# Squares added on GpSimd in pieces of 256 columns, for five head pairs in place of three

## The chip, the core and the metric

The kernel runs on one core of a Trainium2 chip. The metric is the time of one execution on the device in microseconds (us). Five engines work side by side, each through its own list of instructions in order, and wait for each other by semaphores: TensorE (PE in the rows; PEld is its weight load), VectorE (DVE), ScalarE (ACT), GpSimd (POOL) and SyncE (SP), which issues most of the DMA transfers. SBUF is the memory on the core, PSUM holds what TensorE writes.

## The reference

Three layers follow each other. The change lies in the hand-over from the first to the second.

```python
scores = scale * np.matmul(q, k.transpose(0, 1, 3, 2))   # 2 batches, 8 heads, 768 positions, 64 per head
scores = np.where(keep, scores + bias, -1e9)             # window of 96 back, 8 global keys
a = np.exp(scores - max); a = a / (a.sum(-1) + 1e-9)
attn_out = a @ v

x = attn_out.transpose(0, 2, 1, 3).reshape(1536, 512)    # a row: one position, 8 heads of 64
rms = np.sqrt(np.mean(x * x, axis=-1) + 1e-6)            # over the 512 columns of a row
xn = x / rms * rms_g
y = (silu(xn @ w_gate) * (xn @ w_val)) @ w_out           # 512 -> 1536 -> 512

# third layer: tokens routed to one of 8 experts (512 -> 1024 -> 512, relu), added to y
```

`mean(x * x)` is the sum that the change regroups: for each position the squares of 512 numbers are added.

## The kernel before, in words

**Attention.** Work is cut into 24 items: 8 head pairs `pr` (two heads of one batch; `pr` 0 to 3 are batch 0, 4 to 7 batch 1), each with three groups `g` of 256 positions. The generator `attention` runs 28 steps `t`; in step t five items are in flight, each in another stage. For item t (`a`) TensorE multiplies q by k (L243) and VectorE adds the bias and finds the maximum (`ttr`, L254, four instructions); ScalarE takes the exponential with its sum z (`exp`, L265, four). For item t - 1 (`b`) VectorE adds 1e-9 to z and takes the reciprocal (`zadd`, L270; `zrec`, L274) and GpSimd scales the four parts of `es` (`norm`, L282; in step 24, the last with an item `b`, VectorE does it). For item t - 2 (`c`) TensorE transposes (L289), and VectorE and ScalarE copy the result out of PSUM (L298, L300). For item t - 3 (`d`) TensorE multiplies by v (L324). For item t - 4 (`e`) `out` calls `Rms.take`.

**Squares.** `Rms.take` gets 128 partitions (the two heads' 64 columns of x, transposed) by 256 positions. ScalarE scales and rounds them into `xh` (L428), squares them into a third of a tile `sq` of 128 x 768 (L429), and VectorE makes the remainder `xl` (L430). A batch has four such tiles, one for a head pair. The sum over a row's 512 columns is one over 128 partitions and four tiles. `stats` makes it on TensorE: a matmul of a block of 128 positions of `sq` against a column of ones (L458), one for each block and each tile left in the list `self.sq`, 6 blocks in a batch. Each such matmul stands in the trace as two records. `add` (L436) takes the second tile off that list and adds it into the first on GpSimd, 128 x 768 at once; the loop at L401 does it at the end of steps 11, 14 and 23 (head pairs 1, 2 and 5). So batch 0 has two tiles left for `stats`, batch 1 three.

**What follows.** `stats` of batch 0 stands in step 17, of batch 1 in steps 26 and 27. `root` (L461) turns the sums into 1/rms on VectorE in small instructions, one after each of VectorE's other instructions (`tick`); `spread` (L488) brings them to all partitions by TensorE. From step 13 on, one step of a generator `unit` (L498 on) prepares weights of the second layer: ScalarE (L503), VectorE (L505, L510, L512, L515, one in a step), ScalarE (L517) and GpSimd (L518, the low part `wl`). In steps 25, 26 and 27 TensorE begins the second layer's first matmuls (L552).

**Order.** The schedule is by hand: each engine does its instructions in the order in which the program writes them. `sq` has four buffers, which the tiles `rd` of `root` share; a tile's buffer is free when nothing in the program uses it any longer.

Of the kernel before, what the change touches and what calls it, by code (L numbers as in the profile page):

```python
# [15 lines left out]
ALU = mybir.AluOpType  # L16
# [11 lines left out]
def f(ap):  # L28
    return ap.bitcast(F32)
# [162 lines left out]
def attention(s, rms):  # L192
# [11 lines left out]
    def tick():  # L204
        next(s.small, None)


    def load(pr):
        q = qs[pr] = ap.tile([128, 768], F32, name="qd", bufs=3)
        ks[pr] = ap.tile([128, 928], F32, name="kd", bufs=3)  # L210
        if pr:
            nc.sync.dma_start(q, s.qx[pr])
            nc.sync.dma_start(ks[pr], s.kx[pr])
            return
        for a, b, c, d in ((0, 256, 0, 288), (256, 768, 288, 928)):
            nc.sync.dma_start(q[:, a:b], s.qx[pr, :, a:b])
            nc.sync.dma_start(ks[pr][:, c:d], s.kx[pr, :, c:d])

    def loadv(pr):
        v = vs[pr] = ap.tile([128, 2, 11, 64], F32, name="vp", bufs=3)  # L220
        nc.sync.dma_start(v.rearrange("p h b d -> p (h b d)"), s.vx[pr, :, 0:1408])
        lo, hi = halves[pr % 3]
        nc.sync.dma_start(lo[0:64].rearrange("p h b d -> p (h b d)"), s.vx[pr, 0:64, 1408:2176])
        nc.sync.dma_start(hi[64:128].rearrange("p h b d -> p (h b d)"), s.vx[pr, 64:128, 1408:2048])
# [8 lines left out]
    def qk(it, t):  # L233
        pr, g = it

        sc = [s.ps_g.tile([128, 2, 256], F32, name=f"sc{x}", tag=f"ps{x}", bufs=2) for x in range(2)]
        for r in range(2):
            for h, x in ((0, 0), (1, 1), (0, 1), (1, 0)):
                k0, _, _, n = part(g, r, x)
                d = slice(64 * h, 64 * h + 64)  # L240
                o = slice(64 * (h ^ x), 64 * (h ^ x) + 64)
                i = 128 * (2 * g + r) + 64 * x
                nc.tensor.matmul(sc[x][o, r, 0:n], lhsT=qs[pr][d, i:i + 64],  # L243
                                 rhs=ks[pr][d, k0:k0 + n], start=True, stop=True)
        m = ap.tile([128, 4], F32, name="m", bufs=4)
        z = ap.tile([128, 4], F32, name="z", bufs=4)
        st[it] = (sc, es[t % 3], m, z)

    def ttr(it, r, x):

        pr, g = it
        sc, e, m, z = st[it]
        _, b0, e0, n = part(g, r, x)
        nc.vector.tensor_tensor_reduce(  # L254
            out=e[:, r, e0:e0 + n], in0=sc[x][:, r, 0:n], in1=s.bias[:, pr % 4, b0:b0 + n],
            scale=-0.125, scalar=3.0e38, op0=ALU.add, op1=ALU.min,
            accum_out=m[:, 2 * r + x:2 * r + x + 1])

    def exp(it, r):
        pr, g = it  # L260
        sc, e, m, z = st[it]
        for x in range(2):
            _, _, e0, n = part(g, r, x)
            j = 2 * r + x
            nc.scalar.activation(e[:, r, e0:e0 + n], e[:, r, e0:e0 + n], AF.Exp,  # L265
                                 bias=m[:, j:j + 1], scale=-1.0, accum_out=z[:, j:j + 1])

    def zadd(it):
        z = st[it][3]
        nc.vector.tensor_scalar(z, z, 1e-9, None, ALU.add)  # L270

    def zrec(it):
        z = st[it][3]
        nc.vector.reciprocal(z, z)  # L274

    def norm(it, r, x, eng):
        pr, g = it
        sc, e, m, z = st[it]
        _, _, e0, n = part(g, r, x)
        j = 2 * r + x  # L280
        one = (1.0, ALU.mult) if eng is nc.gpsimd else (None,)
        eng.tensor_scalar(e[:, r, e0:e0 + n], e[:, r, e0:e0 + n], z[:, j:j + 1], one[0], ALU.mult, *one[1:])  # L282

    def trans(it, r):
        pr, g = it
        e = st[it][1]
        pt = s.ps_n.tile([128, 3, 128], F32, name="pt", tag="rb", bufs=2)
        for k in range(1 if g == r == 0 else 0, 3):
            nc.tensor.transpose(pt[:, k, :], e[:, r, 128 * k:128 * k + 128], s.ident)  # L289
        pts = ap.tile([128, 3, 128], F32, name="pts", bufs=4)  # L290
        outs[it, r] = (pt, pts)

    def evac(it, r, eng):
        pr, g = it
        pt, pts = outs[it, r]
        k = slice(1 if g == r == 0 else 0, 3)
        if eng is nc.vector:
            nc.vector.tensor_copy(pts[:, k], pt[:, k])  # L298
        else:
            nc.scalar.copy(pts[:, k], pt[:, k])  # L300

    def pv(it, r):
        pr, g = it
        pts = outs.pop((it, r))[1]

        if r == 0:
            po = s.bank([128, 512], "po")
            outs[it] = po[:, 0:256].rearrange("p (a b) -> p a b", a=2)
            s.spare = po[:, 256:512]
        po = outs[it]  # L310
        i = 2 * g + r
        lo, hi = halves[pr % 3]

        def terms(hh):
            a, b = slice(64 * hh, 64 * hh + 64), slice(64 - 64 * hh, 128 - 64 * hh)
            yield 0, 1, lo[:, hh, i], a
            if i:
                yield 0, 0, vs[pr][:, hh, 2 * i - 1], a
                yield 1, 1, hi[:, hh, i - 1], b
            yield 1, 2, vs[pr][:, hh, 2 * i], b  # L320

        for n, two in enumerate(zip(terms(0), terms(1))):
            for hh, (x, k, v, c) in enumerate(two):
                nc.tensor.matmul(po[64 * hh:64 * hh + 64, r, 64 * x:64 * x + 64], lhsT=v,  # L324
                                 rhs=pts[:, k, c], start=i == 0 or n % 2 == 0, stop=i == 0 or n % 2 == 1)

    def out(it):
        pr, g = it
        po = outs.pop(it)
        rms[pr // 4].take(pr % 4, g, po.rearrange("p a b -> p (a b)"))  # L330
# [15 lines left out]
    for t in range(n + 4):  # L346
        a, b, c, d, e = (items[t - z] if 0 <= t - z < n else None for z in range(5))
        if a:
            qk(a, t)
        if c:  # L350
            trans(c, 0)
            trans(c, 1)
        if d:
            pv(d, 0)
            pv(d, 1)
        if b:
            zadd(b)
            tick()
            zrec(b)
            tick()  # L360
            if t < n:
                for r in range(2):
                    for x in range(2):
                        norm(b, r, x, nc.gpsimd)
            else:
                norm(b, 1, 1, nc.vector)
                norm(b, 0, 0, nc.vector)
            tick()
        if a:
            ttr(a, 0, 0)  # L370
            tick()
        if b and t >= n:
            norm(b, 0, 1, nc.vector)
            tick()
        if a:
            ttr(a, 0, 1)
            tick()
            ttr(a, 1, 0)
            tick()
        if b and t >= n:  # L380
            norm(b, 1, 0, nc.vector)
            tick()
        if a:
            ttr(a, 1, 1)
            tick()
        if c:
            evac(c, 0, nc.vector)
        if e:
            out(e)
        for half in range(2):  # L390
            if a:
                exp(a, half)
        if c:
            evac(c, 1, nc.scalar)
        if a:
            pr, g = a
            if g == 1 and pr + 2 < 8:
                load(pr + 2)
            if g == 2 and pr + 2 < 8:
                loadv(pr + 2)  # L400
        for pr in range(8):  # L401
            if pr in (1, 2, 5) and t == 3 * pr + 8:
                rms[pr // 4].add()
        yield t


class Rms:
# [5 lines left out]
    def take(self, hp, g, x):  # L413

        s, nc, b = self.s, self.s.nc, self.b
        if g == 0:
            self.sq.append(s.rpool.tile([128, 768], F32, name="sq", bufs=4))
        self.parts(hp, g, x, self.sq[-1][:, 256 * g:256 * g + 256])

    def place(self, g):  # L420

# [3 lines left out]
    def parts(self, hp, g, x, sq):  # L425
# [3 lines left out]
        nc.scalar.activation(sq, x, AF.Square)  # L429
        nc.vector.scalar_tensor_tensor(out=s.xl[k][:, hp, c], in0=x, scalar=s.rg[:, hp:hp + 1],  # L430
                                       in1=f(s.xh[k][:, hp, c]), op0=ALU.mult, op1=ALU.subtract)

    def add(self):

        sq = self.sq.pop(1)
        self.s.nc.gpsimd.tensor_tensor(self.sq[0], self.sq[0], sq, ALU.add)  # L436

    def general(self, xg):

# [526 lines left out]
def attn_moe_kernel(ctx, tc, qx, kx, vx, rel, ints, wgv, w_out, rms_g, w9, w9t, w1, w2, out):  # L966
# [28 lines left out]

    rms = [Rms(s, 0), Rms(s, 1)]
    att = attention(s, rms)
    ints = load_ints(s)
    s.rel = s.apool.tile([128, 1160], F16, name="rel", bufs=1)
# [282 lines left out]
    def adds():  # L1282
        add(s.x2[9], first[9], start=True)
        add(s.early, s.ident)
        free_wo(0, 3)
# [12 lines left out]
    keep(1)  # L1298
    turn(s, 11, 1)
    add(s.x2[10], first[10], range(2))  # L1300
    logits(s, 11, range(2, 4))
    add(s.x2[10], first[10], range(2, 4))
# [183 lines left out]
```

## Time and profile before

| | |
|---|---|
| runs | 542.07, 548.87, 545.58 us; median 545.58 |
| profiled execution | 542.38 us |
| its span, first to last instruction | 540.6 us |
| busy | PE 95%, PEld 78%, DVE 74%, ACT 50%, POOL 26% |
| granted TensorE clock, mean | 0.996 of full speed |

Busy time is the share of the span in which an engine had an instruction in work; matmul ends are modelled, so a busy PE is not one at its peak. A row of the timeline has the start of an instruction in us from the span's start, its length in us, engine, line, operation, output and input, their size, how many follow each other, and in brackets the engine's idle time before it with what ended that. An instruction that waits for something other than a semaphore stands as a long one.

### The profile page before, as it was taken

The page shows a single profiled execution, that of the slowest core. Times are in us where ns is not written, and L with a number is a line of the kernel's source. Part 1 is how long each engine was busy: PE and PEld are TensorE (multiplying, and loading weights), DVE is VectorE, ACT ScalarE, POOL GpSimd, SP SyncE. Part 2 cuts the span into 40 slices and gives each one's busy share as a digit, 9 for nine tenths or more (in the row PEclk, how much of TensorE's full clock was granted, in tenths as well). Part 3 has the DMA queues.
Part 4 walks back from the last instruction along what each step waited for, and adds up shares of the span by engine and source line. Part 5 has one row for each costly group of instructions (what it writes and reads, how often), then busy time and mean ns, then how long its engine had stood idle before and what let it go on. Part 6 is the DMA issues. An engine that isn't in the chain of part 4 may idle for free. (4 is left out here: it accounts for less than half of the span.)

```text
span 540.6 us, 9830 instructions
## 1 busy us (share of the span) xinstructions
PE 516.0 (95%) x3432; PEld 420.9 (78%) x3432; DVE 402.3 (74%) x1016; ACT 272.1 (50%) x629; POOL 142.1 (26%) x186
## 2 busy tenths in 40 slices
PE   3999997999999999999999999999999999999994
PEld 2676776988888888888888887887898778788873
DVE  5888897578887688768865267767743699999961
ACT  2898895253233332333323343534531679888750
POOL 4557542102221222132212000000000603666001
PEclk9999999999999999999999999999999999999998
DMA  8699701212332323233305323123681799999200
GB/s 253 213 331 280 232 5 39 79 35 89 112 108 88 118 93 102 78 120 115 117 4 194 135 79 117 66 91 118 198 315 40 285 399 396 398 401 392 93 14 18
DMA packets 31001, 85.93 MB, mean 159 GB/s; under 512 B 3847, under 2 KB 4103, under 8 KB 30944
## 3 DMA queue, kind: packets, MB, share of 16 engines
q1 hardware_dynamic: 26400, 73.86, 39.9%
q0 software_dynamic: 2672, 8.22, 4.0%
q10 hardware_dynamic: 1872, 3.15, 1.7%
q8 instruction: 29, 0.48, 0.4%
q14 instruction: 28, 0.23, 0.1%
HBM read 77.52 MB, written 8.65 MB: 159 GB/s over the span
## 5 line engine op out<-in xcount | busy, mean ns | idle before, releaser
L552 PE MATMUL ps<-xh,wh 128*128 128x512 f32 (+1 forms) x304 | 115.4, 379 | 0.1
L552 PE MATMUL ps<-xl,wh 128*128 128x512 f32 (+1 forms) x304 | 114.9, 378 | 0.0
L552 PE MATMUL ps<-xh,wl 128*128 128x512 f32 (+1 forms) x304 | 114.9, 378 | 0.0
L878 DVE TENSOR_TENSOR ewl<-eraw,ewh 128x1024 fp32r<-128x1024 f32 x72 | 83.4, 1214 | 8.1 <-ACT ewh L869 7.7
L869 ACT CAST ewh<-eraw 128x1024 fp32r<-128x1024 f32 x72 | 71.3, 1055 | 6.7 <-DVE ewl L878 6.4
L505 DVE SCALAR_TENSOR_TENSOR wraw<-f64t,wraw 128x512 f32<-128x512 f32 x36 | 44.9, 1248 | 29.0 <-ACT f64t L503 29.0
L552 PEld LDWEIGHTS ps<-xh,wh 128*128 128x128 f32 x304 | 57.2, 188 | 10.8 <-issue 0.2
L552 PEld LDWEIGHTS ps<-xl,wh 128*128 128x128 f32 x304 | 57.2, 188 | 10.6
L552 PEld LDWEIGHTS ps<-xh,wl 128*128 128x128 f32 x304 | 57.2, 188 | 10.6
L628 PE MATMUL px<-woh,hh 128*128 128x512 f32 (+1 forms) x156 | 61.2, 392 | 0.0
L628 PE MATMUL px<-woh,hl 128*128 128x512 f32 (+1 forms) x156 | 58.4, 374 | 0.0
L628 PE MATMUL px<-wol,hh 128*128 128x512 f32 (+1 forms) x156 | 58.2, 373 | 0.0
L518 POOL TENSOR_TENSOR wl<-f64t,wh 128x512 fp32r<-128x512 f32 x24 | 31.0, 1292 | 99.0 <-ACT wh L517 61.1
L517 ACT CAST wh<-f64t 128x512 fp32r<-128x512 f32 x24 | 14.9, 621 | 71.2 <-DVE f64t L515 67.8
L265 ACT ACTIVATE es<-es,m 128x192 f32<-128x192 f32 (+1 forms) x96 | 41.5, 447 | 7.1 <-DVE m L254 7.1
L282 POOL TENSOR_SCALAR es<-es,z 128x192 f32<-128x192 f32 (+1 forms) x92 | 36.1, 411 | 30.8 <-PE pt L289 11.4
L582 DVE TENSOR_TENSOR hl<-h,hh 128x256 fp32r<-128x256 f32 x72 | 25.4, 422 | 17.8 <-ACT hh L581 17.8
L628 PEld LDWEIGHTS px<-woh,hh 128*128 128x128 f32 x156 | 29.4, 188 | 5.6 <-issue 0.9
L628 PEld LDWEIGHTS px<-woh,hl 128*128 128x128 f32 x156 | 29.3, 188 | 5.5
L628 PEld LDWEIGHTS px<-wol,hh 128*128 128x128 f32 x156 | 29.5, 189 | 4.1
L570 DVE TENSOR_TENSOR h<-sg,ps 128x512 f32<-128x512 f32 (+1 forms) x38 | 24.7, 651 | 10.4 <-PE ps L552 8.1
L243 PE MATMUL sc<-kd,qd 64*64 64x192 f32 (+2 forms) x384 | 23.8, 356 | 8.8 <-DVEq L1009 6.9
(208 smaller groups left out, 998.4 us busy)
## 6 DMA issues: line engine op xcount, KB each, us to landing
eraw<-in_w_dram SPq DMA_DIRECT2D x64, 512.0 KB, 9.9
wraw<-in_wgv_dram SPq DMA_DIRECT2D x24, 512.0 KB, 3.8
wraw<-in_w_out_dram SPq DMA_DIRECT2D x12, 512.0 KB, 3.5
vp<-in_vx_dram SPq DMA_DIRECT2D x8, 704.0 KB, 7.4
eraw<-in_w_dram POOLq DMA_DIRECT2D x8, 512.0 KB, 13.5
kd<-in_kx_dram SPq DMA_DIRECT2D x7, 464.0 KB
xm<-x SPq DMA_DIRECT2D x12, 256.0 KB, 2.4
out_dram<-x ACTq DMA_DIRECT2D x12, 256.0 KB
```

What stands on the lines that cost most here:

```text
L243: nc.tensor.matmul(sc[x][o, r, 0:n], lhsT=qs[pr][d, i:i + 64], rhs=ks[pr][d, k0:k0 + n], start=True, stop=True)
L265: nc.scalar.activation(e[:, r, e0:e0 + n], e[:, r, e0:e0 + n], AF.Exp, bias=m[:, j:j + 1], scale=-1.0, accum_out=z[:, j:j + 1])
L282: eng.tensor_scalar(e[:, r, e0:e0 + n], e[:, r, e0:e0 + n], z[:, j:j + 1], one[0], ALU.mult, *one[1:])
L505: nc.vector.scalar_tensor_tensor(out=a.bitcast(F32), in0=t, scalar=F64_LEAST, in1=a.bitcast(F32), op0=ALU.is_ge, op1=ALU.mult)
L517: nc.scalar.copy(hi, t)
L518: eng.tensor_tensor(lo, t, f(hi), ALU.subtract)
L552: nc.tensor.matmul(p, lhsT=w[:, k, :], rhs=x[c][:, k, a:b], start=n == 0, stop=n == 11)
L570: nc.vector.tensor_tensor(u, sg, ps[1], ALU.mult)
L582: nc.vector.tensor_tensor(hl[:, i, :], src, f(hh[:, i, :]), ALU.subtract)
L628: nc.tensor.matmul(p, lhsT=h[:, k, :], rhs=w[k][:, c:c + N], start=n == 0, stop=n == 35)
L869: eng.copy(wh, raw)
L878: eng.tensor_tensor(wl, raw, f(wh), ALU.subtract)
```

## The change

`add` and its calls at steps 11, 14 and 23 go. `take` itself adds on GpSimd, right after it has squared a group of 256 positions: the third of the newest tile into the same third of the batch's first tile. It does so for head pairs 1, 2, 3, 5 and 6, so in steps 7 to 15 and 19 to 24. Batch 0 has one tile left for `stats`, batch 1 two (those of head pairs 4 and 7).

```diff
-        for pr in range(8):
-            if pr in (1, 2, 5) and t == 3 * pr + 8:
-                rms[pr // 4].add()
...
-        self.parts(hp, g, x, self.sq[-1][:, 256 * g:256 * g + 256])
+        c = slice(256 * g, 256 * g + 256)
+        self.parts(hp, g, x, self.sq[-1][:, c])
+        if 4 * self.b + hp in (1, 2, 3, 5, 6):
+            s.nc.gpsimd.tensor_tensor(self.sq[0][:, c], self.sq[0][:, c], self.sq[1][:, c], ALU.add)
+            if g == 2:
+                self.sq.pop(1)
...
-    def add(self):
-
-        sq = self.sq.pop(1)
-        self.s.nc.gpsimd.tensor_tensor(self.sq[0], self.sq[0], sq, ALU.add)
```

GpSimd's list in steps 10 to 12 before (four scalings of a tile `es` in a step, `sq` the squares):

```order
L282 TENSOR_SCALAR es_376<-es_376,z 128x64
L282 TENSOR_SCALAR es_376<-es_376,z 128x128
L282 TENSOR_SCALAR es_376<-es_376,z 128x192 x2
L282 TENSOR_SCALAR es_377<-es_377,z 128x192 x4
L436 TENSOR_TENSOR sq<-sq 128x768
L282 TENSOR_SCALAR es_378<-es_378,z 128x192 x4
```

and the same stretch with the change:

```order
L282 TENSOR_SCALAR es_376<-es_376,z 128x64
L282 TENSOR_SCALAR es_376<-es_376,z 128x128
L282 TENSOR_SCALAR es_376<-es_376,z 128x192 x2
L418 TENSOR_TENSOR sq<-sq 128x256
L282 TENSOR_SCALAR es_377<-es_377,z 128x192 x4
L418 TENSOR_TENSOR sq<-sq 128x256
L282 TENSOR_SCALAR es_378<-es_378,z 128x192 x4
L418 TENSOR_TENSOR sq<-sq 128x256
```

A third of an addition now stands behind the scalings of every step, where a whole one stood behind those of one step in three or more.

GpSimd's list at the end of attention before (the scalings of step 23, then those of the weights):

```order
L518 TENSOR_TENSOR wl_1514<-f64t,wh_1513 128x512
L282 TENSOR_SCALAR es_377<-es_377,z 128x192 x4
L436 TENSOR_TENSOR sq<-sq 128x768
L518 TENSOR_TENSOR wl_1834<-f64t,wh_1833 128x512
L518 TENSOR_TENSOR wl_2004<-f64t,wh_2003 128x512
```

and with the change (lines of the changed file are 3 lower):

```order
L418 TENSOR_TENSOR sq<-sq 128x256
L515 TENSOR_TENSOR wl_1517<-f64t,wh_1516 128x512
L282 TENSOR_SCALAR es_377<-es_377,z 128x192 x4
L418 TENSOR_TENSOR sq<-sq 128x256 x2
L515 TENSOR_TENSOR wl_1841<-f64t,wh_1840 128x512
L515 TENSOR_TENSOR wl_2008<-f64t,wh_2007 128x512
```

Two pieces, of steps 23 and 24, stand where the whole addition stood.

On TensorE nothing moves, but the runs of matmuls against ones are shorter. Its list in step 26 before:

```order
L552 MATMUL ps_1966<-xl_347,wh_1513 128x256
L552 MATMUL ps_1966<-xh_346,wl_1514 128x256
L458 MATMUL ss<-ones,sq 128x1 x12
L552 MATMUL ps_2013<-xh_340,wh_1833 128x512
L552 MATMUL ps_2013<-xl_341,wh_1833 128x512
```

and with the change:

```order
L549 MATMUL ps_1974<-xl_347,wh_1516 128x256
L549 MATMUL ps_1974<-xh_346,wl_1517 128x256
L455 MATMUL ss<-ones,sq 128x1 x8
L549 MATMUL ps_2017<-xh_340,wh_1840 128x512
L549 MATMUL ps_2017<-xl_341,wh_1840 128x512
```

Eight matmuls stand there in place of twelve; in step 27 there are four in place of six, in step 17 six in place of twelve. VectorE's, ScalarE's and SyncE's lists on the way that this input takes stay as they were.

## Rows read from the trace of the kernel before

**Rows 1.** Busy time by stretch: engines, granted clock, DMA share, GB/s.

```profile
22.50:60.50 38.00, 36.24 (x692) 27.03 (x688) 33.40 (x162) 36.48 (x146) 23.37 (x53) 1.00 0.96 289
60.50:86.00 25.50, 22.96 (x374) 17.90 (x372) 22.07 (x101) 23.68 (x88) 14.41 (x29) 1.00 0.28 86
113.00:430.00 317.00, 315.54 (x1547) 261.63 (x1546) 221.78 (x528) 115.88 (x243) 53.19 (x55) 1.00 0.34 117
```

**Rows 2.** Timeline of VectorE, the first instruction of steps 11 to 13.

```profile
40.04 0.17 DVE L270 TENSOR_SCALAR z<-z 128x4 f32<-128x4 f32 x1 [0.36 <-ACT es L265]
42.80 1.25 DVE L270 TENSOR_SCALAR z<-z 128x4 f32<-128x4 f32 x1 [0.50 <-ACT es L265]
46.21 0.17 DVE L270 TENSOR_SCALAR z<-z 128x4 f32<-128x4 f32 x1
```

**Rows 3.** Timeline of GpSimd and ScalarE around the first addition, steps 11 and 12.

```profile
40.62 1.62 POOL L282 TENSOR_SCALAR es<-es,z 128x192 f32<-128x192 f32 x4 [1.29 <-PE pt L289]
42.20 1.82 POOL L436 TENSOR_TENSOR sq<-sq 128x768 f32<-128x768 f32 x1
44.47 0.35 ACT L265 ACTIVATE es<-es,m 128x64 f32<-128x64 f32 x1 [0.65 <-DVE m L254]
```

**Rows 4.** One line's instructions: count, ns least/median/most, first and last start, shape.

```profile
L436 POOL TENSOR_TENSOR sq<-sq x3: 1810/1811/1820, 42.2 to 83.3; 128x768 f32<-128x768 f32 x3
L518 POOL TENSOR_TENSOR wl<-f64t,wh x4: 1268/1281/1292, 62.5 to 102.3; 128x512 fp32r<-128x512 f32 x4
L505 DVE SCALAR_TENSOR_TENSOR wraw<-f64t,wraw x4: 675/986/2032, 51.5 to 98.3; 128x512 f32<-128x512 f32 x4
L282 DVE TENSOR_SCALAR es<-es,z x4: 306/308/2027, 83.2 to 85.6; 128x192 f32<-128x192 f32 x4
```

**Rows 5.** Timeline around the second addition, steps 14 and 15.

```profile
51.12 1.81 POOL L436 TENSOR_TENSOR sq<-sq 128x768 f32<-128x768 f32 x1
51.45 2.03 DVE L505 SCALAR_TENSOR_TENSOR wraw<-f64t,wraw 128x512 f32<-128x512 f32 x1
53.41 0.15 DVE L270 TENSOR_SCALAR z<-z 128x4 f32<-128x4 f32 x1
```

**Rows 6.** Timeline of steps 17 and 18, the sums of batch 0.

```profile
60.48 2.84 PE L458 MATMUL po<-ones,sq 128*128 128x1 f32 x24
62.53 1.27 POOL L518 TENSOR_TENSOR wl<-f64t,wh 128x512 fp32r<-128x512 f32 x1 [1.39 <-ACT wh L517]
63.35 0.17 DVE L465 TENSOR_SCALAR rv<-po 128x6 f32<-128x6 f32 x1 [1.47 <-PE po L458]
```

**Rows 7.** Timeline of step 24, ScalarE and VectorE, under the third addition.

```profile
83.94 0.38 ACT L429 ACTIVATE sq<-po 128x256 f32<-128x256 f32 x1
85.82 0.55 DVE L298 COPY pts<-pt 128x384 f32<-128x384 f32 x1
```

**Rows 8.** Timeline of steps 26 and 27, the sums of batch 1.

```profile
98.03 2.73 PE L458 MATMUL ss<-ones,sq 128*128 128x1 f32 x24
102.31 1.29 POOL L518 TENSOR_TENSOR wl<-f64t,wh 128x512 fp32r<-128x512 f32 x1 [3.27 <-ACT wh L517]
103.89 0.39 PE L552 MATMUL ps<-xh,wl 128*128 128x512 f32 x1
106.17 1.40 PE L458 MATMUL ss<-ones,sq 128*128 128x1 f32 x12
```

**Rows 9.** Timeline of steps 19 to 22, VectorE and GpSimd.

```profile
67.11 1.52 POOL L282 TENSOR_SCALAR es<-es,z 128x64 f32<-128x64 f32 x4 [1.70 <-DVE r L478]
68.61 0.28 DVE L483 TENSOR_SCALAR rd<-ident,r 128x128 f32<-128x128 f32 x1
74.14 1.62 POOL L282 TENSOR_SCALAR es<-es,z 128x192 f32<-128x192 f32 x4 [1.49 <-DVE m L254]
75.67 0.68 DVE L512 SCALAR_TENSOR_TENSOR f64t<-wraw,f64t 128x512 uint32<-128x512 uint32 x1
76.42 0.17 DVE L270 TENSOR_SCALAR z<-z 128x4 f32<-128x4 f32 x1
```

## The prediction, made before the changed kernel was timed

> **What bounds the kernel now.** I read the table of stretches first. From 113 us to 430 us TensorE is busy 315.5 us of 317 at full clock [rows 1]: that part depends on nothing that the change touches, and moves as a whole by what attention gains or loses. The change acts in attention, 22.5 to 86 us, and in the first matmuls behind it. In attention ScalarE is the fullest engine: 36.5 of 38 us up to 60.5 [rows 1]. So a step is worth what ScalarE waits or works in it; it takes 2.76 us where nothing is in the way (40.04 to 42.80) [rows 2].
>
> The second thing to see is a VectorE instruction on four columns, the addition to z, that takes 0.17 us in step 11 and 1.25 us in step 12 [rows 2]. It starts at 42.80 and ends at 44.05, and GpSimd's addition of squares runs from 42.20 to 44.02 [rows 3]. The step after it takes 3.41 us (42.80 to 46.21) [rows 2], and ScalarE's first exponential there has waited 0.65 us for VectorE [rows 3]. The other two additions do the same: L505 takes 2.03 us, its shortest is 0.68 [rows 4, 5]; one of step 24's scalings takes 2.03 us, the others 0.31 [rows 4]. So **each whole addition of 1.81 us holds back one VectorE instruction until it has ended**, and the question is what 15 pieces do in place of 3.
>
> In the sentences of this paragraph I weigh a rule against that. The Trainium skill (SBUF — State Buffer, Who interferes with whom) says that GpSimd shares a pair of ports with VectorE, that whichever starts first has it for its whole instruction and the other stands still, and that on VectorE's side this meets the 2-port modes, which a tensor_scalar can enter, and instructions with two inputs in SBUF. The three blocked instructions above are of those kinds, and none ends before the addition that it met, so the trace agrees. The rule speaks against this change, since 15 pieces hold the pair longer than 3 whole additions: if what is blocked grew as the time for which the pair is held, 11.3 us for 5.4, the 1.08 + 1.35 + 1.72 us blocked now would become 8.7, and the kernel would take 546.9 us.
>
> **A piece.** No row shows 256 columns. An addition of 768 takes 1.811 us, a subtraction of 512 takes 1.281 [rows 4]; the line through them gives 2.07 ns a column and 0.75 us for 256. From below it is 1.811 / 3 = 0.60, from above 1.28, if columns below 512 save nothing. I take 0.75. Fifteen are 11.3 us of GpSimd in place of 5.4. GpSimd has room (23.4 of 38 us busy [rows 1]); what counts is whom a piece meets.
>
> **Gains.**
> (a) Step 11's whole addition goes: 0.65 us, what ScalarE waited [rows 3].
> (b) Step 14's goes, a piece stays there, from 51.12 to 51.87. L505 began at 51.45 and ended at 53.48, 0.55 us behind the addition's end at 52.93 [rows 5]; 0.55 behind the piece is 52.42, so VectorE wins 1.06. ScalarE's own work covers some of it, so I take 0.6 (0 to 1.06).
> (c) Step 17 has 12 records fewer of 24 that took 2.84 us [rows 6]: 1.4 us. VectorE's `rv` waits 1.47 us for them. But next GpSimd subtracts weights until 63.80 [rows 6], its scalings of step 18 are queued behind that, and by what was seen above it holds back `root`'s instructions with two inputs. I take 0.45 (0 to 1.4).
> (d) Step 24: the whole addition from 83.28 cost one scaling 2.03 - 0.31 = 1.72 us [rows 4], and VectorE's copy, for which TensorE waits, came at 85.82 [rows 7]. Now one piece follows the scalings at 83.28 and ends at 84.03; the other needs the square that ends at 83.94 + 0.38 = 84.32 [rows 7], so a scaling gets in between. I take 0.5 (0.2, the saving of 1.81 against two pieces and some, to 1.2, if all scalings get ahead of the second piece).
> (e) Steps 26 and 27: 12 records fewer of 36 that took 2.73 + 1.40 us [rows 8]: 1.37 us of an engine that has nothing else to wait for. But after step 26 TensorE needs `wl` of the fourth weight unit, which lands at 102.31 + 1.29 = 103.60, and the matmul that reads it starts at 103.89 [rows 8]. That chain does not hang on the sums, so of 0.91 us there some 0.23 remain (0.29 less the hand-over); the 0.46 of step 27 remain whole. I take 0.7 (0.46 to 1.37).
> Together 2.9 us (1.3 to 5.7).
>
> **Losses.**
> (f) Steps 7 to 10, 12 and 13. In step 11 the addition starts 42.20 - 40.04 = 2.16 us after the step's z [rows 2, 3]; a piece would end at 2.91, and a blocked z ends 0.03 us after what blocks it (44.05 against 44.02). So the next z would end 2.94 us after this one's start, and unblocked 2.76 + 0.17 = 2.93. **Piece and z just pass each other.** I take 0.2 us for the six together. Where z does come late, ScalarE covers some: 1.08 us of delay in step 12 became 0.65 of waiting, so 0.4 is slack.
> (g) Step 15: the same picture with one more VectorE instruction: 0.2.
> (h) Steps 19 to 22. Here VectorE does `root`'s and the weights' instructions late in a step. In step 19 the scalings end at 67.11 + 1.52 = 68.63 and a `rd` instruction is due at 68.61 [rows 9]: a toss, up to 0.75; I take 0.55. In step 21 L512 starts at 75.67, before the scalings end at 75.76, so the piece waits for it until 76.35 and ends at 77.10; z, due at 76.42 [rows 9], waits 0.7, of which ScalarE covers some: 0.4. Steps 20 and 22, whose rows are like these, 0.35 together. In all 1.3.
> Together 1.7 us (0, if every piece falls between; 13 x 0.75 = 9.8, if each of the pieces before step 23 costs its length).
>
> Costed at nothing: the new waits of squares for GpSimd, since those buffers were read by additions four steps back or more, and the wait of a piece for its square, which in step 24's row ends 0.38 us behind its start and elsewhere comes while GpSimd still scales.
>
> **The sum.** -2.9 + 1.7 = -1.2 us. The profiled execution took 542.38 us with a span of 540.6: it would take 541.2. The runs shown lie at 542.07, 545.58 and 548.87; the profiled one stands near their lowest, 3.2 below their median. New runs fall between, so I add half of that: **542.8 us**. A difference under 2% (10.9 us) is about what a measurement of this kernel can tell from no change; nothing above comes near it.
>
> **Rivals.**
> First, **the pieces fall between and the shorter sums count in full**: gains at their upper ends, no losses, 5.7 us: 536.7 us by the profiled execution. For it: a piece that meets nothing costs nothing, and (f) is that close. Against it: the fourth weight unit in (e) does not come earlier. 0.17.
> Second, slower: **the piece takes the place of ScalarE as what sets the step.** From z to scalings, to the piece, to the next z is then a ring through VectorE and GpSimd. It takes 2.94 - 0.17 = 2.77 us at 0.75 for a piece, against 2.76 us of ScalarE. Each 0.1 us more in a piece is 0.1 us more in every step; it decides from about 0.75 us in long runs of steps, and at once where a piece exceeds 0.75 by the slack of 0.4. At 1.28 us a piece, 13 x 0.53 = 6.9 us come on top of (f) to (h): 542.38 - 1.2 + 6.9 = 548.1 us. For it: steps 7 to 15 are nine in a row, so small delays add up; VectorE's list is full in steps 19 to 22. Against it: two points give a straight line for a piece. The rule of the Trainium skill named above (SBUF — State Buffer, Who interferes with whom) is what closes this ring. 0.28.
> The forecast 0.55.
>
> **How the numbers follow.** The forecast's own range is 539 to 545.5: losses and gains of some 1.5 us each way, and where a run lies among runs. The first rival reaches 537 or so, the second 548 and, with a run on the slow side, 550. I leave out what lies beyond **538 to 548.5**. Faster by over 2% would need twice the first rival's gain: 0.02. Slower by over 2% needs every piece to cost its length and more: 0.03. Within 2%: 0.95.
>
> **What would show it.** The pieces' own rows: 0.75 us each, 15 of them. The z instruction of steps 7 to 15: about 0.17 to 0.3 us, and steps of 2.76 us; z at 0.5 us and more in every step, and steps of 3 us, would be the second rival. Step 12 to 13 back at 2.76 us. L505 in step 14 at 1.1 us. `rv` of batch 0 some 1.4 us earlier, and the first exponential of step 18 only 0.45 earlier. Steps 19 and 21 longer by 0.4 to 0.6. The sums of batch 1 as 16 records of 1.85 us and 8 of 0.9, and a wait of TensorE for `wl` of some 0.7 us between them. The end of `root` about 1.2 us earlier than now, and everything from 113 us on moved by that and unchanged. I would be wrong if a piece takes much more than 0.75 us, if the pair goes to VectorE's next instruction before a waiting piece, or if the later part does not move with attention's end.

## The result: 0.992 of the time before, about half of it by TensorE's clock

| | before | with the change |
|---|---|---|
| first comparison, 8 runs each | 545.43 us (541.91 to 548.87) | 542.26 us (538.98 to 542.87) |
| ratio, 95% interval | | 0.9917 (0.9889 to 0.9945) |
| profiled execution, span, mean granted clock | 542.38, 540.6, 0.996 | 542.6, 540.8, 0.991 |
| second trace of the same kernel (from the experiments) | 547.52, 545.7, 0.987 | 540.15, 538.3, 0.997 |

The ratio stands for -4.5 us (-3.0 to -6.1), within the 2% that I took as no change; the forecast was 542.8 us. The two profiled executions alone would say that nothing happened (542.38 and 542.6). The clock of each explains that, as the rows show.

**The profile after.** First the table of stretches that answers to [rows 1], with five finer stretches (columns as there: PE, PEld, DVE, ACT, POOL busy, granted clock, DMA):

```profile
22.50:60.50 38.00, 36.73 (x703) 27.79 (x701) 32.54 (x166) 37.17 (x149) 26.38 (x60) 1.00 0.92 283
60.50:86.00 25.50, 22.07 (x361) 17.12 (x362) 23.94 (x102) 23.67 (x87) 17.16 (x34) 0.96 0.28 86
113.00:430.00 317.00, 315.26 (x1545) 261.46 (x1546) 221.95 (x528) 115.62 (x245) 52.91 (x54) 1.00 0.34 116
82.00:84.00 2.00, 1.54 (x14) 0.98 (x15) 1.19 (x3) 2.00 (x8) 1.97 (x5) 0.96 0.25 88
84.00:86.00 2.00, 1.38 (x23) 1.19 (x22) 2.00 (x6) 1.39 (x5) 0.73 (x1) 0.50 0.00 0
86.00:88.00 2.00, 2.00 (x20) 1.67 (x21) 1.99 (x5) 0.48 (x1) 0.00 (x0) 0.50 0.00 0
88.00:90.00 2.00, 2.00 (x26) 1.79 (x23) 0.01 (x1) 0.71 (x2) 0.00 (x0) 0.50 0.00 0
90.00:92.00 2.00, 2.00 (x8) 1.58 (x8) 1.08 (x2) 1.31 (x2) 0.00 (x0) 0.83 0.00 0
```

From 113 to 430 us nothing changed. From 84 to 90 us TensorE was granted half of its clock, 1.2 GHz, which the trace of before never shows in attention. I call such a stretch a fall of the clock. Next the pieces and the instructions that they met, VectorE's and GpSimd's timelines (lines are 3 lower than before from L401 on):

```profile
L418 POOL TENSOR_TENSOR sq<-sq x15: 719/727/1202, 31.9 to 84.4; 128x256 f32<-128x256 f32 x15
```

```profile
40.75 0.17 DVE L270 TENSOR_SCALAR z<-z 128x4 f32<-128x4 f32 x1 [0.24 <-ACT es L265]
43.50 0.17 DVE L270 TENSOR_SCALAR z<-z 128x4 f32<-128x4 f32 x1 [0.50 <-ACT es L265]
46.61 0.17 DVE L270 TENSOR_SCALAR z<-z 128x4 f32<-128x4 f32 x1
51.85 0.97 DVE L502 SCALAR_TENSOR_TENSOR wraw<-f64t,wraw 128x512 f32<-128x512 f32 x1
55.29 0.57 DVE L270 TENSOR_SCALAR z<-z 128x4 f32<-128x4 f32 x1
61.86 0.17 DVE L462 TENSOR_SCALAR rv<-po 128x6 f32<-128x6 f32 x1
```

```profile
54.90 0.93 POOL L418 TENSOR_TENSOR sq<-sq 128x256 f32<-128x256 f32 x1
75.33 1.20 POOL L418 TENSOR_TENSOR sq<-sq 128x256 f32<-128x256 f32 x1
```

The z of step 12 is back at 0.17 us [rows 2]; L502 of step 14 takes 0.97, not 2.03 [rows 5]. The z of step 16 is held back by a piece: it ends at 55.86, the piece at 55.83. So are those of steps 10 and 22, which take 0.33 and 0.70 us. The sums, on TensorE, answer to [rows 6, 8]:

```profile
60.32 1.50 PE L455 MATMUL po<-ones,sq 128*128 128x1 f32 x12
99.62 1.84 PE L455 MATMUL ss<-ones,sq 128*128 128x1 f32 x16
105.22 0.50 PE L549 MATMUL ps<-xh,wl 128*128 128x512 f32 x1 [0.47 <-POOL wl L515]
107.65 0.95 PE L455 MATMUL ss<-ones,sq 128*128 128x1 f32 x8
```

### The profile page after: what moved, and what is told of

It is laid out like the page before. It is cut to its first block, busy times and chain, and to the rows that moved or that the text cites. A ratio compares the mean times of both kernels' runs of the same rounds, so it can differ in the third digit from the quotient of the medians.

```text
span 540.8 us, 9801 instructions
## 1 busy us (share of the span) xinstructions
PE 516.5 (96%) x3408; PEld 420.9 (78%) x3408; DVE 402.2 (74%) x1016; ACT 272.4 (50%) x629; POOL 147.9 (27%) x198
## 3 DMA queue, kind: packets, MB, share of 16 engines
q10 hardware_dynamic: 1872, 3.15, 1.7%
## 5 line engine op out<-in xcount | busy, mean ns | idle before, releaser
L502 DVE SCALAR_TENSOR_TENSOR wraw<-f64t,wraw 128x512 f32<-128x512 f32 x36 | 43.9, 1219 | 28.8 <-ACT f64t L500 28.8
```

The costliest lines, as they stand in the source:

```text
L502: nc.vector.scalar_tensor_tensor(out=a.bitcast(F32), in0=t, scalar=F64_LEAST, in1=a.bitcast(F32), op0=ALU.is_ge, op1=ALU.mult)
```

## The experiments

Each ran against the kernel before on the same chip; ratios carry their 95% interval. The mean granted clock of the whole execution is given as "clock".

**1 to 4: additions and sums apart.** All start from the change or from before; lines of `take`:

```diff
 none_long  (the change without the piece; pops pairs 1, 2, 5)
-            s.nc.gpsimd.tensor_tensor(self.sq[0][:, c], self.sq[0][:, c], self.sq[1][:, c], ALU.add)
+        if 4 * self.b + hp in (1, 2, 5) and g == 2:
             self.sq.pop(1)
 none_short  (the same, pops pairs 1, 2, 3, 5, 6)
 whole_short  (before, whole additions kept)
+        if 4 * self.b + hp in (3, 6) and g == 2:
+            self.sq.pop()
 pieces15_long  (the change, pops only pairs 1, 2, 5)
-            if g == 2:
+            if g == 2 and hp + 4 * self.b in (1, 2, 5):
                 self.sq.pop(1)
```

Expected: 

> No addition of squares on GpSimd at all; the sums read as many tiles as before (2 and 3), so the squares of head pairs 1, 2 and 5 are left out of the sums. All times against the kernel before. By the terms of the prediction (blocked VectorE instructions a, b, d cost 1.75 us, sums c, e 1.15, new pieces 1.7): -1.75 us. If the shorter sums alone bring the change its gain (about 3 us) and additions hide: 0 us. If the whole additions alone cost it: -3 us.

> No addition on GpSimd at all, and the sums as short as with the change (1 and 2 tiles); the squares of pairs 1, 2, 3, 5 and 6 are left out. Against the kernel before: by the terms of the prediction -2.9 us; this is also the change without the cost of its 15 pieces, so it should lie 1.7 us under the change. If the pieces hide altogether: equal to the change. In both rivals (sums alone, whole additions alone) about -3 us, equal to the change.

> The three whole additions as before, but the sums as short as with the change: the squares of pairs 3 and 6 are left out. Against the kernel before: by the terms of the prediction -1.15 us (c and e alone); if the shorter sums alone bring the gain: -3 us, equal to the change; if the whole additions cost it: 0 us.

> The 15 pieces of the change, but the sums as long as before: the tiles of pairs 3 and 6 stay in the sums and count twice. Against the kernel before: by the terms of the prediction -0.05 us (1.75 won, 1.7 lost); if the shorter sums alone bring the gain: 0 us; if the whole additions cost it and pieces hide: -3 us, equal to the change.

| | sums | median us | ratio to before | clock, median |
|---|---|---|---|---|
| none_long | long | 542.65 | 0.9913 (0.9881 to 0.9944) | 0.991 |
| none_short | short | 539.62 | 0.9866 (0.9836 to 0.9897) | 0.997 |
| whole_short | short | 542.01 | 0.9919 (0.9889 to 0.9949) | 0.994 |
| pieces15_long | long | 545.78 | 1.0006 (0.9979 to 1.0033) | 0.987 |

Fifteen pieces for three whole additions are worth nothing (pieces15_long), as forecast at -0.05; shorter sums alone bring -4.4 us (whole_short), all that the change brings and far over my 1.15. The two kernels without any addition leave out squares and show what the additions cost. Both missed: none_long gains 4.7 us (3.1 to 6.5), where the prediction's terms said 1.75 and no rival more than 3; none_short gains 7.3 for 2.9, and lies 2.8 us under the change, not 1.7. But the removed records last only 2.68 us (1.34, 0.89 and 0.45 less in the rows above than in [rows 6, 8]), so their time cannot be all. The clock column is higher with the short sums, and higher too without the additions (0.991 in none_long, whose sums are long). The trace of pieces15_long shows one place, TensorE alone (busy, granted clock, DMA); its run, 541.78 us at 0.994, is the fastest of twelve, whose median clock is 0.987, so most of them lost more:

```profile
59.00:62.00 3.00, 3.00 (x46) 1.00 0.39 113
62.00:64.00 2.00, 2.00 (x22) 0.56 0.98 322
64.00:66.00 2.00, 2.00 (x28) 0.59 1.01 291
```

```profile
59.59 2.91 PE L455 MATMUL po<-ones,sq 128*128 128x1 f32 x24
```

The 24 one-column records end at 62.50, and there the clock goes to half. That is a second theory, which the prediction has no term for: **the sums act on the clock**.

**5 to 8: is it the clock, and what brings it down?**

before_again is the kernel before. before_split breaks the run of step 17's sums:

```diff
             pv(d, 0)
+            if t == 17:
+                rms[0].stats(0)
             pv(d, 1)
+            if t == 17:
+                rms[0].stats(1)
...
+        if t == 18:
+            rms[0].stats(2)
+            s.small = rms[0].root()
```

change_long17 keeps pair 3's tile in step 17's sums (`if g == 2 and hp != 3`); change_fill adds matmuls behind `pv(d, 1)`:

```diff
+            for _ in range({22: 2, 23: 5, 24: 4}.get(t, 0)):
+                nc.tensor.matmul(s.spare[:, 0:128], lhsT=s.ident, rhs=s.ones, start=True, stop=True)
```

Expected: 

> The kernel before once more, for a second trace. Among 17 more runs of it the mean granted clock was 0.996 in the two at 542 us, 0.991 in two at 544 to 545, and 0.986 to 0.990 in most, at 545.5 to 547.5 us. If the granted clock in attention is what parts these runs, its trace has stretches at half clock between 40 and 92 us, most of all behind the 24 sum records of step 17 (about 63 to 66 us), where two traces with 24 such records show them, and none elsewhere; each costs about 2 us. If its runs differ by something else (transfers, waits), a trace at 545 us or more shows the clock as in the first trace (1.00 from 22 to 510 us).

> The kernel before with the same 24 one-column records for batch 0, in three pieces of 8 with other matmuls between them: one between the two halves of step 17's multiplication by v, one behind it, one in step 18 behind q by k. If the unbroken run of one-column matmuls is what the fall of the clock follows, -2 to -3 us against before, with a mean clock of 0.991 or more in most runs. If only the time of the records counts: 0 to +1 us, since rv starts some 1.5 us later, and a mean clock as before.

> The change, but step 17 sums two tiles as before (24 records; the squares of pair 3 count twice), steps 26 and 27 as with the change. If the change wins mainly by the clock behind the shorter run of step 17: +2 to +4 us against the change (543.5 to 546 us), mean clock 0.984 to 0.990 in most runs, and a stretch at half clock at 62 to 66 us in the trace. If only the time of the 12 records counts: +0.45 (prediction) to +1.4 us (all of it), and a mean clock as with the change, 0.991 to 0.995.

> The change with 2, 5 and 4 matmuls of 128x128 more at the ends of steps 22, 23 and 24, whose result nobody reads; TensorE waits 1.05 and 0.62 us behind steps 23 and 24 in the change's trace. If the fall of the clock at 84 to 91 us in the change's trace follows TensorE's idle time at 78 to 86: no fall there, mean clock 0.995 in nearly all runs, 539 to 540.5 us, about 2 us less than the change. If it is not that: the same clock as the change, and 0 to +0.8 us for what the matmuls hold back.

| | median us | ratio to before | clock, median |
|---|---|---|---|
| before_again | 545.90 | 1.0013 (0.9979 to 1.0048) | 0.990 |
| before_split | 544.62 | 0.9992 (0.9959 to 1.0024) | 0.991 |
| change_long17 | 543.21 | 0.9968 (0.9939 to 0.9997) | 0.994 |
| change_fill | 541.10 | 0.9918 (0.9892 to 0.9944) | 0.996 |

The second trace of before, TensorE alone:

```profile
62.00:64.00 2.00, 2.00 (x20) 1.00 0.60 163
64.00:66.00 2.00, 2.00 (x22) 0.53 1.02 361
66.00:68.00 2.00, 2.00 (x28) 0.61 0.86 285
86.00:88.00 2.00, 0.75 (x24) 1.00 0.01 2
88.00:90.00 2.00, 1.49 (x8) 0.51 0.00 0
90.00:92.00 2.00, 2.00 (x34) 0.64 0.00 0
104.00:106.00 2.00, 2.00 (x9) 0.77 0.02 8
106.00:108.00 2.00, 2.00 (x7) 0.50 0.68 240
108.00:110.00 2.00, 2.00 (x9) 0.87 0.04 14
```

and what TensorE did ahead of the first, second and third fall, in its timeline:

```profile
61.56 2.96 PE L458 MATMUL po<-ones,sq 128*128 128x1 f32 x24
88.51 1.54 PE L289 MATMUL pt<-ident,es 128*128 128x128 f32 x6 [1.76 <-DVE pts L298]
101.44 2.73 PE L458 MATMUL ss<-ones,sq 128*128 128x1 f32 x24
```

This is one kernel, twice: without a fall (540.6 us, the trace that I predicted from) and with three (545.7). Two follow 24 sum records, one a wait of 1.76 us. But the first trace has all three as well, the 24 records in 2.84 and 2.73 us [rows 6, 8] and this wait, and its clock stays at 1.00:

```profile
86.42 0.88 PE L289 MATMUL pt<-ident,es 128*128 128x128 f32 x6 [1.77 <-DVE pts L298]
```

So none of them brings a fall by itself, and what differs between the two executions no row shows. Against the first trace, the z of step 18 stands 1.08 us later (62.79 for 61.71), before any fall; that of step 24 2.09 later (84.86 for 82.77), the first weight matmul 3.40 (91.71 for 88.31), the second sums 5.02 (111.19 for 106.17). So the three falls cost 1.0, 1.3 and 1.6 us.

Splitting the run did not help: the ratio is 1, and its trace falls to half at 64 to 70 us. That reason, the unbroken run, fell. change_long17 stands 0.0051 above the change's ratio (2.8 us, by two sessions whose intervals are 1.6 us each way). Its trace falls behind the 24 records (0.50 at 64 to 66 us), but most of its runs have 0.994 and four 0.983 to 0.989, where the clock theory had forecast 0.984 to 0.990 in most: right in direction, too large in size. In change_fill the fall at 84 to 91 is gone:

```profile
80.70 1.38 PE L357 MATMUL po<-ones,ident 128*128 128x128 f32 x10
81.92 0.65 PE L289 MATMUL pt<-ident,es 128*128 128x128 f32 x3
84.16 1.16 PE L357 MATMUL po<-ones,ident 128*128 128x128 f32 x8
```

```profile
82.00:84.00 2.00, 1.76 (x30) 1.00 0.11 43
84.00:86.00 2.00, 1.92 (x22) 1.00 0.00 0
```

and no run is under 0.993, but by the ratio the time equals the change's: of the 2 us expected nothing showed.

**9 to 12: the clock held up on both sides.** before_fill_wide and change_fill_wide are before and the change with these edits; before_wide has the second alone; change_again is the change:

```diff
+            for _ in range({23: 5, 24: 4}.get(t, 0)):
+                nc.tensor.matmul(s.spare[:, 0:128], lhsT=s.ident, rhs=s.ones, start=True, stop=True)
...
-                nc.tensor.matmul(self.ss[:, j:j + 1], lhsT=sq[:, 128 * j:128 * j + 128], rhs=s.ones[:, 0:1],
+                nc.tensor.matmul(self.ss[:, 32 * j:32 * j + 32], lhsT=sq[:, 128 * j:128 * j + 128], rhs=s.ones[:, 0:32],
```

Expected: 

> The change once more, beside the next two. By the first comparison: 542.3 us, 0.992 of before. If the granted clock parts its runs as it did there: 539 to 540.2 us where the mean clock is 0.995, 542 to 543 where it is 0.991 to 0.994.

> The kernel before, all its additions and all its sum records kept, with two edits for TensorE alone: each sum record is 32 columns wide in place of one (its result stands 32 times, one is read), and 5 and 4 idle matmuls of 128x128 stand at the ends of steps 23 and 24. If most of the difference between before and the change is the granted clock: no stretch at half clock at 62 to 68 and 84 to 92 us, mean clock 0.994 to 0.997, 542 to 543.5 us, -3 to -4 against before. If the clock is a by-thing and the time of the sums and the blocked instructions decide: 0 to +1 against before (545.5 to 547.5 us).

> The change with the same two edits. Against before_fill_wide it shows what additions and sums are worth with the clock up on both sides: -1.2 us by the sum of the prediction, about -2.5 by the runs at equal mean clock so far (542.2 at 0.996 before, 539.6 at 0.995 with the change). If the clock were no part of it, the full -4. Against the change itself: -1.5 to -2 if the fall at 84 to 91 us goes away and the idle matmuls hold back nothing; 0 or more if they do.

> The kernel before with the wide sum records alone (32 columns, one read), without the idle matmuls of steps 23 and 24. If the narrow records of step 17 bring the fall at 62 to 68 us and TensorE's idle time in steps 23 and 24 the one at 84 to 92: no half clock at 62 to 68, mean clock 0.990 to 0.994 in most runs, 543.5 to 545 us, between before (546.3) and the version with both edits (542.9). If the wide records do all of it: 542.9 and 0.996 to 0.997. If the idle matmuls did all of it: as before, with half clock at 62 to 68.

| | median us | ratio to before | clock, median |
|---|---|---|---|
| change_again | 540.42 | 0.9928 (0.9899 to 0.9957) | 0.995 |
| before_fill_wide | 542.86 | 0.9962 (0.9934 to 0.9991) | 0.997 |
| change_fill_wide | 540.66 | 0.9920 (0.9892 to 0.9949) | 0.996 |
| before_wide | 545.01 | 0.9976 (0.9953 to 1.0000) | 0.991 |

before_fill_wide does all that before does and more, and its median is 3.45 us lower than before's in the same session (546.31; by the ratio -2.1, -0.5 to -3.6); 11 of its 12 runs have a clock of 0.996 to 0.998. **With the clock up on both sides the change is worth 542.86 - 540.66 = 2.2 us** (0.9 to 2.5 when the 12 and 12 runs are drawn anew). The change gains nothing from the same edits (540.42 and 540.66): it already has most of what they give. change_again parts its runs by the clock as expected: 539.5 to 541.1 us at 0.995 and more (eight), 542.4 to 542.7 at 0.989 to 0.993 (three), 544.8 at 0.988.

before_wide missed its expectation at one point: behind 24 records of 32 columns its clock still falls, and behind the same 24 in before_fill_wide it does not. First before_wide, then before_fill_wide:

```profile
64.00:66.00 2.00, 2.00 (x25) 0.79 1.04 322
66.00:68.00 2.00, 2.00 (x28) 0.50 0.99 230
```

```profile
64.00:66.00 2.00, 2.00 (x35) 1.00 0.97 324
66.00:68.00 2.00, 2.00 (x43) 1.00 0.86 283
```

So the wide records alone did not keep the clock up (two of 12 runs have 0.996), and the idle matmuls of steps 23 and 24, which stand 20 us later, go with a fall that is gone at 64. No run shows how; the two ran on different chips, but before has 0.988 or less in most runs on both; the idle matmuls on before without the wide records were not tried. What the 14 traces do show is a count. Behind 24 records in step 17 the clock falls in 6 of 8 (not in the first of before, nor in before_fill_wide), behind 12 in none of 6. Behind the 24 records of step 26 it falls in one of 7. At 82 to 96 us it falls in 5 of 11 without idle matmuls and in none of 3 with them. That holding the clock up saves time is shown; what starts a fall stays open.

## Why the prediction was right, and which of its steps were not

The second trace of the change has no fall in attention, nor has the first of before: these two can be compared step by step. Times are between starts of z, to the first weight matmul, and to `rv` of batch 1.

| stretch | before | change | difference | term, forecast |
|---|---|---|---|---|
| z of step 6 to 12 | 16.20 | 16.24 | +0.04 | (f), +0.2 with 13 to 14 |
| 12 to 13 | 3.41 | 2.60 | -0.81 | (a) -0.65 |
| 13 to 14 | 2.75 | 2.78 | +0.03 | (f) |
| 14 to 15 | 4.45 | 3.38 | -1.07 | (b) -0.6 |
| 15 to 18 | 8.30 | 8.85 | +0.55 | (g) +0.2 |
| 18 to 19 | 4.84 | 4.09 | -0.75 | (c) -0.45 |
| 19 to 23 | 13.06 | 13.95 | +0.89 | (h) +1.3 |
| 23 to 24 | 3.16 | 3.15 | -0.01 | |
| 24 to weight matmul | 5.54 | 4.93 | -0.61 | (d) -0.5 |
| that to `rv` | 19.38 | 18.84 | -0.54 | (e) -0.7 |
| sum | 81.09 | 78.81 | **-2.28** | -1.2 |

These rows of the second trace carry it (z of steps 6, 12, 13, 14, 15, 18, 19 and 22, and step 24's copy):

```profile
27.51 0.17 DVE L270 TENSOR_SCALAR z<-z 128x4 f32<-128x4 f32 x1 [0.37 <-ACT es L265]
43.75 0.17 DVE L270 TENSOR_SCALAR z<-z 128x4 f32<-128x4 f32 x1 [0.51 <-ACT es L265]
46.35 0.33 DVE L270 TENSOR_SCALAR z<-z 128x4 f32<-128x4 f32 x1 [0.41 <-ACT es L265]
49.13 0.17 DVE L270 TENSOR_SCALAR z<-z 128x4 f32<-128x4 f32 x1 [0.23 <-ACT es L265]
52.51 0.16 DVE L270 TENSOR_SCALAR z<-z 128x4 f32<-128x4 f32 x1
61.36 0.16 DVE L270 TENSOR_SCALAR z<-z 128x4 f32<-128x4 f32 x1
65.45 0.15 DVE L270 TENSOR_SCALAR z<-z 128x4 f32<-128x4 f32 x1
75.65 0.70 DVE L270 TENSOR_SCALAR z<-z 128x4 f32<-128x4 f32 x1
85.00 0.55 DVE L298 COPY pts<-pt 128x384 f32<-128x384 f32 x1
```

and these of before, steps 14, 18 and 19 (others stand in [rows 2, 5, 9]):

```profile
48.96 0.17 DVE L270 TENSOR_SCALAR z<-z 128x4 f32<-128x4 f32 x1 [0.37 <-ACT es L265]
61.71 0.17 DVE L270 TENSOR_SCALAR z<-z 128x4 f32<-128x4 f32 x1
66.55 0.15 DVE L270 TENSOR_SCALAR z<-z 128x4 f32<-128x4 f32 x1
```

- **The mechanism held.** The terms have their signs, and 2.28 is what the runs with the clock up give (2.2). That the two spans differ by 2.3 as well is in part chance: outside the table the change's trace reaches step 6 0.91 us later and is 0.93 shorter behind `rv`, and behind the second layer (410 us) the 14 traces take 129.7 to 131.1 us with no order by kernel. (a) is 0.30 in the first trace (43.50 to 46.61), where TensorE stood idle for 0.65 us at 43.06 with nothing in the profile to wait for, and 0.81 in the second, without that stop.
- **(b) was mis-sized by most**: all of the 1.06 us that VectorE won came out at the end of the step. I had let ScalarE's work cover some 0.46 of it; it covered none.
- **(c)**: `rv` came 1.49 us earlier in the first trace (61.86 for 63.35), and the stretch from step 18 to 19 is 0.75 shorter, not 0.45. whole_short shows the same stretch at 4.09 us with the additions left whole: it is the sums' alone. **(e)**: the wait for `wl` is there, 0.47 us in the row. From the first sums to the second TensorE takes 8.03 us (97.21 to 105.24) for 8.14 before, so of the 0.89 saved there 0.11 remain, where I said some 0.23; the rest of the term is step 27.
- **The losses** are 1.5 us for the 1.7 forecast, (g) larger than told and (h) smaller. The wait of step 21 came as told: the piece lasts 1.20 us in the first trace, and the z behind it takes 0.70, not 0.17. Against none_short, which has no additions, the change still loses 1.10 us in step 24 alone (4.93 to 3.83, from 80.50 to the weight matmul at 84.33).
- **The rivals.** The ring of piece and z did not close: a piece takes 0.727 us, and steps 7 to 12 last as long as before. That rival is out, and so is the first, whose full 1.37 us for (e) came as 0.54. The Trainium skill (SBUF — State Buffer, Who interferes with whom) lets one engine hold the shared ports for a whole instruction; the blocked z that ends 0.03 us behind its piece agrees. That the loss would grow with the time held, 546.9 us, did not come. In the second trace ten of the 15 pieces lengthen a VectorE instruction, but by short amounts: 4.35 us in all over the same instructions in none_short, for 4.15 blocked before, while the pieces hold GpSimd for 11.6 us in place of 5.4.

**The step that failed is the baseline.** I took the profiled execution, 542.38, for one of a spread, and added half of its distance to the median as "where a run lies among runs". That spread is the clock. Of 97 more runs of before only 12 have a mean clock of 0.996 (median 542.1), 57 have 0.988 or less (546.9). Of 20 runs of the change 11 have 0.995 or more (540.0), 8 have 0.989 to 0.994 (542.5), one 0.988 (544.8). So the change gains twice: 2.1 us between the runs without falls (542.1 to 540.0), and some 2 us because falls are fewer, for which no term stood. That the forecast of 542.8 was met by 542.26 is luck, since two misses cancel: 540.1 by the rows (542.38 - 2.28), and 2.2 us for a fall as in its first trace, whose `rv` of batch 1 stands 2.41 us later than the second's (108.73 for 106.32), 0.19 of it before step 24. Five of its first eight runs have the clock that goes with it.

## What to carry to other kernels

Where runs of one kernel lie 1% apart, ask first whether the profiled one is typical: look at its mean granted clock beside that of the others, and at half clock in stretches of 2 us. A change can be worth as much by the clock that it leaves to TensorE as by the time of the instructions that it removes, and then a trace of one execution of each can show neither. To part the two, hold the clock up on both sides, or compare only traces without a fall.

## What the runs showed of the hardware

- TensorE's clock fell to half while its records show it busy without a gap: 2.00 of 2 us at 62 to 64 and at 64 to 66 in the second trace of before, behind 24 one-column records. The Trainium skill (TensorE: Matmul & The Clock Gate, Part 1: The HAM clock gate (the "warmup" mystery)) ties the clock to how busy the array has lately been and warns of idle gaps: the fall behind the wait of 1.76 us is of that kind, but a wait of 1.77 us at the same place in the first trace had none behind it, and the fall behind the sums has no gap in the rows.
- A fall cost 1.0 to 1.6 us in the second trace of before, the longer one of 84 to 91 us in the change's first trace 2.2. none_long has one at 46 to 48 us (0.50), after TensorE stood idle for 0.65 us with nothing in the profile to wait for and 0.90 us for a transfer of k.
- A record of 32 columns is as long as one of a single column: 24 took 2.87 us (before_fill_wide) and 2.84 (before).
- Executions of one kernel part before the change: the z of step 6 stands at 26.60 us in the first trace of before, at 27.62 in the second.
